# Gated decode attention with a GLU branch: where W_gate and W_up stand among the first loads

## The chip, the core and the metric

The kernel runs on one core of a Trainium2 chip. The metric is the device time of one execution in microseconds (us); lower is better. Three runs of the kernel before gave 1275.69, 1276.04 and 1276.13 us, a median of 1276.04 us.

## The reference

One token passes through two branches, and a scalar gate mixes them. All inputs are bfloat16.

```python
def _A_ref(x, k_cache, v_cache, wq, wo):      # x [1,1,448]; 16 query heads, 8 KV heads, Sk 65536, Dh 256
    q = (x @ wq).reshape(B, Sq, Hq, Dh).transpose(0, 2, 1, 3)
    ...                                       # each KV head serves 2 query heads
    scores = jnp.einsum("bhqd,bhkd->bhqk", q, k) * (Dh ** -0.5)
    p = _softmax(scores, axis=-1)
    o = jnp.einsum("bhqk,bhkd->bhqd", p, v)
    return o.transpose(0, 2, 1, 3).reshape(B, Sq, Hq * Dh) @ wo
def _B_ref(x, W_gate, W_up, W_down):          # W_gate, W_up [448,1792]; W_down [1792,448]
    gate = x @ W_gate; up = x @ W_up
    return (gate * (gate > 0) * up) @ W_down
g = _sigmoid((x * gate_w).sum(-1, keepdims=True))
return g * a + (1 - g) * b
```

The K and V caches hold 8 x 65536 x 256 values each, 537 MB together. Everything else is small beside them.

## The kernel before

**Tiles.** Each KV head h has four K tiles and four V tiles. A tile is 16384 rows of 256 values, laid out as 128 partitions by 32768 values, 8192 KB. In all there are 32 K tiles (k0 to k31, called n in the code) and 32 V tiles (v0 to v31).

**Three slots.** A tile fills one of three SBUF buffers, `ring[0]` to `ring[2]`. K tile n goes to slot 1 + n % 2. V tiles go to slot 0, apart from the last four. Slot 0 has other guests before v0 comes: the query weights (the load `wq`, in the two pieces L626 and L627), W_down behind them (`wd`, L675), and then, over the place of the query weights, W_gate and W_up (`gu`, two DMAs each, L640 and L642). A load into a slot waits for the last reader of what lay there (`free`): k2 waits for the scores of k0, k3 for those of k1, k4 for those of k2. The `gu` loads wait for the query projection `q`, which reads the query weights. v0 waits for the whole GLU branch, since `gu`'s data and its intermediate results lie in slot 0.

**One queue of loads.** All these loads are issued by SyncE (SP) in one fixed order. SP waits for the semaphores of one load, issues it, and goes on to the next; a load that waits holds up those behind it.

**Work on a tile.** For a K tile, VectorE transposes it in place in four steps (L529), TensorE multiplies each half with the query (`qk[n, 0]` and `qk[n, 1]`, L540), VectorE takes the maximum of the scores (L703), and ScalarE the exponential (L705). When the four K tiles of a head are done, the head's softmax factors follow (L715 to L760). For a V tile, ScalarE brings the tile's weights into place (`pc`, L591) and TensorE multiplies (`pv`, L584). The GLU branch runs once, after the scores of k2: the products with W_gate and W_up on TensorE (`f_gu`, L653), relu, product, transpose and cast on VectorE (L659, L660, L663, L664), and the product with W_down on TensorE (`f_dn`, L551 with `hT`, in the code `dn`).

**What sets the order.** A planner written by hand. The list `order` names the loads with an estimated duration each; their running sum gives each load a planned issue time `t` and a planned landing time `tL`. Each operation gets a key worked out from these times, and each engine's program is sorted by key. So the list sets the order on SP directly, and the order on the other engines by the keys. Dependencies become semaphore waits afterwards.

Of the kernel before, what the change touches and what calls it, by code (L numbers as in the profile page):

```python
# [27 lines left out]
class _Plan:  # L28
# [8 lines left out]
    def op(self, eng, key, fn, deps=(), tag=None):  # L37
        eng, cls = {"pv": ("pe", "pv"), "dx": ("dv", "dx"), "ap": ("ac", "ap")}.get(eng, (eng, eng))
        o = _Op(eng, key, fn, deps, tag=tag, cls=cls)
        self.ops.append(o)  # L40
        return o
# [219 lines left out]
def bass_gated_mix__gqa_block_cached__glu_gated_reglu__decode_kernel(  # L261
# [35 lines left out]
    with es:  # L297
# [73 lines left out]
        op, dma = pl.op, pl.dma  # L371
# [6 lines left out]


        TILE = 19.35  # L380
        order = [("k", 0, TILE), ("wq", 0, 8.7), ("k", 1, TILE), ("wd", 0, 3.8), ("k", 2, TILE), ("gu", 0, 7.7)]
        for n in range(3, NT):
            order.append(("k", n, TILE))
            if n >= NTH:
# [10 lines left out]
        t = 3.0  # L395
        tL, issue = {}, []
# [158 lines left out]
        def f_sel(e, win):  # L555
            for d_ in range(8):
                ins = e.matmul(AX_ps, win(d_), o_sb[:, d_ * 32:(d_ + 1) * 32],
                               start=False, stop=False, skip_group_check=True)
            return ins

        l_, qk, smax, aexp, pv, pc, last, first = {}, {}, {}, {}, {}, {}, {}, {}
# [8 lines left out]
        def zero_o(key, h):  # L570
            last["zo", h] = op("pv", key, lambda e: e.matmul(
                OP[:], identb[:, :], zer[:, 0:1].to_broadcast([128, 512]), start=True, stop=True, skip_group_check=True),
                [c_ze, g_idb, l_["hT"], last.get(("o1", h - 1))], tag="zo")

        def make_pv(n, lo, hi, sl, tv, dep):
            h, a = divmod(n, NTH)

            def f_pv(lo, hi):
                return lambda e: f_mm(e, lo, hi)

            def f_mm(e, lo, hi):
                for k in range(lo // 2, hi // 2):
                    g = k % 4
                    ins = e.matmul(OP[32 * g:32 * g + 4, :], pcur[a % 2][:, 4 * k:4 * k + 4],  # L584
                                   ring[sl][:, k * 512:(k + 1) * 512],
                                   start=False, stop=False, skip_group_check=True,
                                   tile_position=(0, 32 * g))
                return ins
            tp = max(tv, last["tev", h])
            if lo == 0:  # L590
                pc[n] = op("ap", max(tp - 5, last["tev", h] - 0.5), lambda e: e.copy(  # L591
                    pcur[a % 2][:].rearrange("p (k i) -> p k i", i=4),
                    ptp[:].rearrange("p (k i f) -> p k i f", i=4, f=4)[:, :, :, a]), last["ev", h] + [pv.get(n - 2)])
            if lo == 0 and a == 0:
                zero_o(last["tev", h] - 0.3, h)
            if n < NT - 1:
                pc[n].deps.append(dep)
            deps = ([dep] if n == NT - 1 else []) + [pc[n]] + ([last["zo", h]] if a == 0 and lo == 0 else [])
            if n >= NT - NTH and a == 1:
                for q_, (l2, h2) in enumerate(PIECES):  # L600
                    pv[n] = op("pv", tp + 0.1 * q_, f_pv(l2, h2), deps if q_ == 0 else [pc[n]], tag=("tail", 1, q_))
            else:
                tag = ("pv", a % 2, sl) if n < NT - NTH else ("tail", a % 2, 0 if n < NT - 1 else [q_[0] for q_ in PIECES].index(lo))
                pv[n] = op("pv", tp, f_pv(lo, hi), deps, tag=tag)
            if a == NTH - 1 and hi == U:
                tn = last["T", h + 1] + 18.5 if n < NT - 1 else tp + 1.2
                o1 = op("dx", tn, lambda e: e.tensor_scalar(o_sb[:], OP[:, 0:256], rcm[:, 0:1], None, ALU.mult),  # L607
                        [pv[n], last.get(("otr", h - 1)), last["rc", h]])
                last["ocp", h] = o1
                o1 = op("dx", tn + 0.05, lambda e: e.scalar_tensor_tensor(  # L610
                    o_sb[:], OP[:, 256:512], rcm[:, 1:2], o_sb[:], ALU.mult, ALU.add), [o1, last.get(("ec", h))])

                if h < H - 1:
                    o2 = op("pv", tn + 0.3, lambda e: f_sel(e, lambda d_: ecur[:, 7 - d_:135 - d_]),
                            [o1], tag="otr")
                else:
                    o2 = op("pv", tn + 0.5, lambda e: f_sel(e, lambda d_: esel[:, 120 - 16 * h - d_:248 - 16 * h - d_]),
                            [o1, g_es, l_["axz"]])
                if h < H - 1:
                    last["l5", h + 1].deps.append(o1)  # L620
                last["o1", h], last["otr", h] = o1, o2
                last["tn", h] = tn + 1

        for kind, i, t in sorted(issue, key=lambda q: q[0] != "wq"):
            if kind == "wq":
                l_["wq"] = dma("sp", t, "wq", lambda e: e.dma_start(wq3, A_wq[0:NR3, :].rearrange("(p k) n -> p (k n)", k=R3)))  # L626
                l_["wqh"] = dma("sp", t + 0.01, "wqh", lambda e: e.dma_start(wqh, A_wq[NR3:D, :].rearrange("r (t n) -> (r t) n", t=2)))  # L627
# [48 lines left out]
            elif kind == "k":  # L676
                n = i
                h, t_ = divmod(n, NTH)
# [29 lines left out]
                if t_ == NTH - 1:  # L708
# [18 lines left out]
                    for rd in range(2):  # L727
# [18 lines left out]
                        q = op("ac", tt + 1, f_ev, [p, pv.get((h - 1) * NTH - 1)])  # L746
# [18 lines left out]
                    for args in [p_ for p_ in pending if p_[0] // NTH == h]:  # L765
                        make_pv(*args)
                        pending.remove(args)
            elif kind in ("v", "vp"):
                if kind == "v":
                    n, lo, hi = i, 0, U  # L770
                    sl = slot["v", n]
                    dep = dma("sp", t, "r%d" % sl, lambda e, sl=sl, n=n: e.dma_start(ring[sl][:], v_src(n)), free(("v", n)))
                else:
                    n, (lo, hi) = NT - 1, PIECES[i]
                    sl = slot["vp", 0]
                    dep = dma("sp", t, ("wq", "wqh", "wd")[i], lambda e, sl=sl, n=n, lo=lo, hi=hi: e.dma_start(  # L776
                        ring[sl][:, lo * 256:hi * 256], v_src(n)[:, :, lo * 256:hi * 256]), free(("vp", 0)))
                args = (n, lo, hi, sl, tL[kind, i], dep)
                if ("tev", n // NTH) in last:
                    make_pv(*args)  # L780
                else:
                    pending.append(args)
            elif kind == "wo":
                lo, hi = WO[i]
                l_["wo", i] = dma("sp", t, "wo%d" % i, lambda e, lo=lo, hi=hi: e.dma_start(  # L785
                    wo_sb[:, lo:hi, :], A_wo.rearrange("(p s) n -> p s n", s=32)[:, lo:hi, :]), free(("wo", 0)))
# [89 lines left out]
```

## Time and profile before

| | |
|---|---|
| median of 3 runs | 1276.04 us (1275.69 to 1276.13) |
| span of the profiled execution | 1274.3 us |
| DMA: share of 16 engines' span, bytes, mean rate | 99.7%, 549.13 MB, 431 GB/s |
| VectorE (DVE) busy | 630.1 us (49%) |
| TensorE (PE) busy | 365.9 us (29%) |
| ScalarE (ACT) busy | 78.0 us (6%) |

The page gives the profiled execution's span and no other time of its own; the span is 1.7 us below the median of the three runs, and that difference lies around the span. Times within the profile are us from the start of the span. "DMA ring<-in_A_k_cache_dram" is the load of a K tile, "SPq" is SP's queue of DMA issues. The number that stands for a DMA "to landing" runs from the start of its issue until its semaphore shows that all of it has arrived. An entry in square brackets behind an instruction is the idle time of its engine before it, and what ended it.

### The profile page before, as it was taken

The numbers are of one execution on the slowest core, as the hardware profiler recorded it, in microseconds if no ns is written. First come the engines' busy times: TensorE is split into PE (matmuls) and PEld (weight loads), VectorE is DVE, ScalarE is ACT, GpSimd is POOL, SyncE is SP. The second block draws the span as 40 slices with busy tenths as digits, with TensorE's granted clock in tenths as the row PEclk, the third lists the DMA queues.
The fourth block names the chain that finished last, engine by engine and source line by source line (L and its number), as shares of the span: only waits on it lengthen the run. The fifth ranks groups of instructions, "written<-read, shape, count | busy, mean of one in ns | idle before, by whom it ended". The sixth has DMA issues, their size and how long they took to land.

```text
span 1274.3 us, 10240 instructions
## 1 busy us (share of the span) xinstructions
PE 365.9 (29%) x4497; PEld 151.4 (12%) x4505; DVE 630.1 (49%) x309; ACT 78.0 (6%) x163; POOL 4.6 (0%) x23
## 2 busy tenths in 40 slices
PE   0534321133320332312233222323302332112525
PEld 0101110011110111101111110111100111001201
DVE  4777655553455633557433565335654355553300
ACT  0001100010000100001000010000000010000100
POOL 1000000000000000000000000000000000000000
PEclk9766665666655666656666656666566666566667
DMA  9999999999999999999999999999999999999998
GB/s 411 430 436 432 426 430 434 432 443 432 430 432 432 434 442 430 430 434 430 438 438 430 430 434 430 440 438 428 430 434 430 444 434 428 430 436 430 442 421 369
DMA packets 11389, 549.13 MB, mean 431 GB/s; under 512 B 1267, under 2 KB 1654, under 8 KB 2294
## 3 DMA queue, kind: packets, MB, share of 16 engines
q1 hardware_dynamic: 11378, 549.03, 99.7%
q8 instruction: 4, 0.07, 0.0%
q14 instruction: 3, 0.02, 0.0%
q10 hardware_dynamic: 4, 0.00, 0.0%
HBM read 549.03 MB, written 0.00 MB: 431 GB/s over the span
## 4 chain that ended last, share of the span: by engine, by line
DMA 81%; PE 16%; DVE 2%; ACT 1%; issue 1%; SPq 0%; ACTq 0%
DMA ring<-in_A_v_cache_dram 74%; PE O L584 13%; DMA ring<-in_A_wo_dram 3%; DMA ring<-in_A_wq_dram 2%; DMA ring<-in_A_k_cache_dram 2%; DVE ring L529 1%; PE ST L540 1%; ACT pcur L591 1%; PE O L501 1%; PE A_ps L551 0%; SPq L785 0%; SPq L776 0%; PE O L653 0%; DVE ring L660 0%; PE A_ps L653 0%
## 5 line engine op out<-in xcount | busy, mean ns | idle before, releaser
L529 DVE STREAM_TRANSPOSE ring<-ring 128x4096 uint32<-128x4096 uint32 x128 | 557.6, 4413 | 196.9 <-DMA ring<-in_A_k_cache_dram 196.9
L584 PE MATMUL O<-ring,pcur 128*4 128x512 bf16 x2048 | 187.3, 545 | 790.4 <-ACT pcur L591 781.9
L703 DVE TENSOR_REDUCE nmb<-ST 128x1 f32<-128x512 f32 x32 | 22.1, 692 | 345.9 <-PE ST L540 345.9
L584 PEld LDWEIGHTS O<-ring,pcur 128*4 128x4 bf16 x2048 | 59.3, 111 | 914.8 <-ACT pcur L591 794.6
L540 PE MATMUL ST<-ring,xcur 128*16 128x512 bf16 x2048 | 136.7, 420 | 44.3 <-DVE ring L529 43.7
L540 PEld LDWEIGHTS ST<-ring,xcur 128*16 128x16 bf16 x2048 | 62.4, 92 | 112.1 <-DVE ring L529 48.6
L705 ACT ACTIVATE P_sb<-ST,nmb 128x512 bf16<-128x512 f32 x32 | 44.6, 1392 | 368.3 <-DVE nmb L703 368.3
L591 ACT COPY pcur<-ptp 128x256 bf16<-128x256 bf16 x32 | 13.2, 415 | 732.6 <-DMA ring<-in_A_v_cache_dram 732.6
L607 DVE TENSOR_SCALAR o_sb<-O,rcm 128x256 bf16<-128x256 f32 x8 | 3.8, 479 | 61.1 <-PE O L584 61.1
L730 DVE TENSOR_TENSOR P_sb<-P_sb,hs 128x1024 bf16<-128x1024 bf16 x16 | 18.9, 1222 | 8.1 <-ACT hs L724 8.1
L735 PE MATMUL PT<-identb,P_sb 128*128 128x128 bf16 x128 | 14.5, 282 | 17.6 <-DVE P_sb L730 17.3
L501 PE MATMUL O<-ring,P_sb 128*128 128x512 bf16 x28 | 8.5, 477 | 17.3 <-DMA ring<-in_A_wq_dram 17.3
L735 PEld LDWEIGHTS PT<-identb,P_sb 128*128 128x128 bf16 x128 | 10.7, 127 | 19.9 <-DVE P_sb L730 19.9
L744 ACT COPY ptp<-PT 128x256 bf16<-128x256 bf16 x32 | 10.3, 375 | 23.0 <-PE PT L735 23.0
L705 ACT ACTIVATION_READ_ACCUMULATOR P_sb<-ST,nmb 128x1 f32 x32 | 8.3, 258 | 0.0
L501 PEld LDWEIGHTS O<-ring,P_sb 128*128 128x128 bf16 x28 | 3.2, 117 | 22.2 <-issue 20.5
L551 PE MATMUL A_ps<-ring,attnA 128*1 128x224 bf16 x64 | 5.3, 322 | 1.1 <-DMA ring<-in_A_wo_dram 1.0
L719 PE MATMUL M_ps<-identf,hs 128*2 128x128 f32 x8 | 2.3, 283 | 10.0 <-DVE hs L717 10.0
L756 DVE RECIPROCAL rc<-M_ps 128x2 f32<-128x2 f32 x8 | 1.4, 171 | 7.5 <-PE M_ps L755 7.5
L755 PE MATMUL M_ps<-hs,ones_f 128*128 128x2 f32 x16 | 4.5, 352 | 0.0
L722 PE MATMUL M_ps<-mx,nselT 2*128 2x1 f32 x16 | 3.2, 268 | 3.0 <-DVE mx L721 3.0
L755 PEld LDWEIGHTS M_ps<-hs,ones_f 128*128 128x128 f32 x16 | 4.0, 311 | 0.0
(93 smaller groups left out, 68.6 us busy)
## 6 DMA issues: line engine op xcount, KB each, us to landing
ring<-in_A_v_cache_dram SPq DMA_DIRECT2D x1, 4096.0 KB, 22.1
ring<-in_A_wq_dram SPq DMA_DIRECT2D x1, 3072.0 KB, 28.9
ring<-in_A_v_cache_dram SPq DMA_DIRECT2D x1, 3072.0 KB, 28.8
ring<-in_B_W_down_dram SPq DMA_DIRECT2D x1, 1568.0 KB, 53.0
ring<-in_B_W_gate_dram SPq DMA_DIRECT2D x1, 1344.0 KB, 26.3
ring<-in_B_W_up_dram SPq DMA_DIRECT2D x1, 1344.0 KB, 29.2
ring<-in_A_wo_dram SPq DMA_DIRECT2D x1, 1232.0 KB, 33.0
ring<-in_A_v_cache_dram SPq DMA_DIRECT2D x1, 1024.0 KB, 30.7
```

What stands on the lines that cost most here:

```text
L501: ins = e.matmul(QN_ps, xw3[:, kt, 31 - m:159 - m], rhs, start=(kt == 0 and m == 0), stop=(kt == R3 and m == J // 4 - 1))
L529: return lambda e: e.transpose(v, v)
L540: ins = e.matmul(bank[32 * w:32 * w + 16, :], xcur[:, x0:x0 + 16], ktv[sl][:, u0:u0 + 16, c, :, r_], start=(b == 0 and c == 0 and r_ == 0) ...
L551: ins = e.matmul(A_ps[32 * g:32 * g + 1, 0:D2], lhsT, rhs[:, g * D2:(g + 1) * D2], start=start, stop=stop, skip_group_check=True, tile_pos ...
L584: ins = e.matmul(OP[32 * g:32 * g + 4, :], pcur[a % 2][:, 4 * k:4 * k + 4], ring[sl][:, k * 512:(k + 1) * 512], start=False, stop=False, s ...
L591: pc[n] = op("ap", max(tp - 5, last["tev", h] - 0.5), lambda e: e.copy(pcur[a % 2][:].rearrange("p (k i) -> p k i", i=4), ptp[:].rearrange ...
L703: smax[n] = op("dv", sx, lambda e, n=n, t_=t_: e.tensor_reduce(NM[:, t_:t_ + 1], ST[n % 2][:], AX.X, ALU.max, negate=True), [qk[n, 1], las ...
L705: aexp[n] = op("ac", sx + 1, lambda e, n=n, t_=t_: e.activation(P_sb[:, t_:2048:4], ST[n % 2][:], ACTF.Exp, bias=NM[:, t_:t_ + 1], scale=1 ...
L730: rsc = op("dv", tt, lambda e, pb=pb: e.tensor_tensor(pb, pb, X[:, 12:16].unsqueeze(1).to_broadcast([128, 256, 4]), ALU.mult), [h7, aexp[n]])
L735: ins = e.transpose(PT[rd][:, s * 128:(s + 1) * 128], P_sb[:, (rd * 8 + s) * 128:(rd * 8 + s + 1) * 128], identb[:, :])
L744: ins = e.copy(dst, src)
L755: l3 = mop("pe", T + 19, lambda e: e.matmul(LS_ps, ones_f[:, :], X[:, 6:8], start=True, stop=True), [l2, c_one], tag="l3")
```

## The change

W_gate and W_up are loaded ahead of the third K tile, k2; they came behind it. The list `order` says so. Two more lines keep the rest in place: the GLU operations are still created after k2's (so that they can refer to the scores of k2), and the first V tile's weight copy `pc[0]` gets a key that leaves it where it was on ScalarE.

```diff
-        order = [("k", 0, TILE), ("wq", 0, 8.7), ("k", 1, TILE), ("wd", 0, 3.8), ("k", 2, TILE), ("gu", 0, 7.7)]
+        order = [("k", 0, TILE), ("wq", 0, 8.7), ("k", 1, TILE), ("wd", 0, 3.8), ("gu", 0, 7.7), ("k", 2, TILE)]
...
-                pc[n] = op("ap", max(tp - 5, last["tev", h] - 0.5), lambda e: e.copy(
+                pc[n] = op("ap", max(tp - (5 if n else 1), last["tev", h] - 0.5), lambda e: e.copy(
...
-        for kind, i, t in sorted(issue, key=lambda q: q[0] != "wq"):
+        for kind, i, t in sorted(issue, key=lambda q: (q[0] != "wq", tL["k", 2] if q[0] == "gu" else q[2])):
```

On SP, the first loads of the program before stand as follows; k0 and the query weights are ahead of this piece, the first row is k1, and `s_pe` and `s_pv` are the semaphores of TensorE's score products and of its other products.

```order
L680 DMA ring<-in_A_k_cache_dram 128x32768
L675 DMA ring<-in_B_W_down_dram 128x6272
L680 DMA ring<-in_A_k_cache_dram 128x32768 [waits s_pe]
L640 DMA ring<-in_B_W_gate_dram 128x5376 [waits s_pv]
L642 DMA ring<-in_B_W_gate_dram 128x896
L640 DMA ring<-in_B_W_up_dram 128x5376
L642 DMA ring<-in_B_W_up_dram 128x896
L680 DMA ring<-in_A_k_cache_dram 128x32768 [waits s_pe] x2
L772 DMA ring<-in_A_v_cache_dram 128x1x32768 [waits s_pv]
```

The same piece of SP's program after the change:

```order
L680 DMA ring<-in_A_k_cache_dram 128x32768
L675 DMA ring<-in_B_W_down_dram 128x6272
L640 DMA ring<-in_B_W_gate_dram 128x5376 [waits s_pv]
L642 DMA ring<-in_B_W_gate_dram 128x896
L640 DMA ring<-in_B_W_up_dram 128x5376
L642 DMA ring<-in_B_W_up_dram 128x896
L680 DMA ring<-in_A_k_cache_dram 128x32768 [waits s_pe] x3
L772 DMA ring<-in_A_v_cache_dram 128x1x32768 [waits s_pv]
```

k2 has moved behind the four loads of W_gate and W_up; it is now the first of the three K tiles (k2, k3, k4) that stand in one row ahead of v0. Nothing else moves on SP.

On VectorE, the program from the maximum of k1's scores to the transposes of k3 is the same before and after the change (`d_r1` and `d_r2` are the landings in slots 1 and 2, `s_pv` at L659 the products with W_gate and W_up):

```order
L703 TENSOR_REDUCE nmb<-ST 128x1 [waits s_pe]
L529 STREAM_TRANSPOSE ring<-ring 128x4096 [waits d_r1]
L529 STREAM_TRANSPOSE ring<-ring 128x4096 [waits s_ac]
L529 STREAM_TRANSPOSE ring<-ring 128x4096 x2
L703 TENSOR_REDUCE nmb<-ST 128x1 [waits s_pe]
L659 TENSOR_SCALAR ring<-O 128x448 [waits s_pv]
L660 SCALAR_TENSOR_TENSOR ring<-ring,gb,A_ps 128x448 [waits s_dx]
L663 STREAM_TRANSPOSE ring<-ring 128x448 [waits s_dx]
L664 CAST hT<-ring 128x14 [waits s_dx]
L529 STREAM_TRANSPOSE ring<-ring 128x4096 [waits d_r2]
```

The first transposes are k2's, the last row is k3's first; the GLU steps stand between them, so they still run after the scores of k2, wherever their data has arrived by then. TensorE's and ScalarE's programs are also the same as before.

## The prediction

> **What bounds the kernel now.** I read the page first, for the share of each resource, and then SP's waits, the chain of waits, and the timelines of SP, DVE and PE over the first 160 us, where the change lies. From the page, the span, the DMA rate in 40 slices, and the queue that the loads use:
>
> ```profile
> span 1274.3 us, 10240 instructions
> GB/s 411 430 436 432 426 430 434 432 443 432 430 432 432 434 442 430 430 434 430 438 438 430 430 434 430 440 438 428 430 434 430 444 434 428 430 436 430 442 421 369
> q1 hardware_dynamic: 11378, 549.03, 99.7%
> ```
>
> The 16 DMA engines work for 99.7% of the span, and the rate is level from the second slice to the last but one. The kernel is a queue of loads that never runs dry. Its length is bytes by rate; other work counts only where it lets the queue run dry, and such a gap is then never made up, since no later stretch has spare rate. The change neither adds nor removes a byte. So there is one question: does the new order of issue open or close a gap?
>
> The table of windows gives the rate of the steady part (its last three columns are PE's granted clock, the DMA share and GB/s), and the chain of waits, below it, the pace of its tiles (start, duration):
>
> ```profile
> 141.10:1231.70 1090.60, 302.26 (x3915) 127.49 (x3922) 531.26 (x229) 66.76 (x140) 0.00 (x0) 0.62 1.00 434
> ```
>
> ```profile
> 141.18 0.43 ACT pcur L591
> ...
> 1224.80 0.42 ACT pcur L591
> ```
>
> The DMA share there is 1.00 and the rate 434 GB/s, so nothing can go faster there. Between v0's landing (the copy at 141.18) and v28's (1224.80) lie 28 pairs of a K and a V tile, so a pair takes 38.70 us and **one tile 19.35 us** of the queue.
>
> Next, SP's timeline: when each load is issued (start, duration of the issue).
>
> ```profile
> 0.72 0.42 SPq L680 DMA_DIRECT2D ring<-in_A_k_cache_dram  x1
> 2.71 0.53 SPq L675 DMA_DIRECT2D ring<-in_B_W_down_dram  x1
> 50.70 0.33 SPq L680 DMA_DIRECT2D ring<-in_A_k_cache_dram  x1
> 52.56 0.44 SPq L642 DMA_DIRECT2D ring<-in_B_W_up_dram  x1
> 73.23 0.33 SPq L680 DMA_DIRECT2D ring<-in_A_k_cache_dram  x1
> 96.48 0.33 SPq L680 DMA_DIRECT2D ring<-in_A_k_cache_dram  x1
> 104.18 0.64 SPq L772 DMA_DIRECT2D ring<-in_A_v_cache_dram  x1
> 123.51 0.34 SPq L680 DMA_DIRECT2D ring<-in_A_k_cache_dram  x1
> ```
>
> These are k0, W_down, k2, the last piece of W_up, k3, k4, v0 and k5. The DMA view, asked for the issue of one load at a time, gives the time from issue to landing; its rows for k0, W_down, the last piece of W_up, k2, k3 and k4 are:
>
> ```profile
> ring<-in_A_k_cache_dram SPq DMA_DIRECT2D x1, 22.1
> ring<-in_B_W_down_dram SPq DMA_DIRECT2D x1, 1568.0 KB, 53.0
> ring<-in_B_W_up_dram SPq DMA_DIRECT2D x1, 224.0 KB, 30.5
> ring<-in_A_k_cache_dram SPq DMA_DIRECT2D x1, 24.6
> ring<-in_A_k_cache_dram SPq DMA_DIRECT2D x1, 29.1
> ring<-in_A_k_cache_dram SPq DMA_DIRECT2D x1, 25.3
> ```
>
> Adding these to the issues: W_down lands at 55.7, k2 at 75.3, W_up at 83.1, k3 at 102.3 and k4 at 121.8. The steps after W_down are 19.6, 7.8, 19.2 and 19.5, each what its bytes need. So the queue is fed without a gap through this part, and the slack of a load is the time between its issue and the landing of the load ahead of it: k2 is issued 5.0 us before W_down lands, k3 9.9 us before W_up lands, and **k4 5.8 us before k3 lands** (102.3 less 96.48).
>
> What releases k4 is seen in the chain of waits (start, duration), and on DVE's timeline:
>
> ```profile
> 31.49 8.51 PE O L501 x28
> ...
> 50.70 24.64 DMA ring<-in_A_k_cache_dram
> 75.37 17.43 DVE ring L529 x4
> 92.85 3.59 PE ST L540 x30
> ...
> 101.00 0.18 DVE hT L664
> ...
> 104.18 36.90 DMA ring<-in_A_v_cache_dram
> ...
> 147.16 32.62 DMA ring<-in_A_v_cache_dram
> ```
>
> ```profile
> 96.49 0.69 DVE L703 TENSOR_REDUCE nmb<-ST 128x1 f32<-128x512 f32 x1 [3.70 <-PE ST L540]
> 102.40 17.42 DVE L529 STREAM_TRANSPOSE ring<-ring 128x4096 uint32<-128x4096 uint32 x4 [1.22 <-DMA ring<-in_A_k_cache_dram]
> 131.30 17.42 DVE L529 STREAM_TRANSPOSE ring<-ring 128x4096 uint32<-128x4096 uint32 x4
> ```
>
> k2 lands, four transposes take 17.4 us, the second half of its scores 3.6 us, and with that its slot is free and k4 is issued: 96.48 less 75.34, 21.1 us after the landing.
>
> **The change, part by part.**
>
> *W_gate and W_up go earlier.* They wait only for the query projection, whose 28 products end at 40.0 (31.49 and 8.51). Their four issues now run then, not from 51.08. SP has nothing to do until 50.70, so no other load is held up by that wait. k1 and W_down are in the queue until 55.7, so the four loads land behind them, at about 55.7 + 7.7 = 63.4. Nobody wants them then: the GLU products stand on PE behind k2's scores, as before. Gain: nothing, for nobody waited for them at 83.1 either; the products began as k2's scores ended.
>
> *k2 goes later.* It is still issued at 50.70, when k0's scores are done, but lies behind W_gate and W_up. It lands where W_up landed, at 83.1, which is **7.7 us later** (83.06 less 75.34; their 3136 KB at 434 GB/s would be 7.4).
>
> *k3 stays.* Its issue at 73.23 hangs on the scores of k1, which the change does not touch. It is now 9.8 us ahead of k2's landing, and lands at 102.3 as before, since the bytes ahead of it are the same.
>
> *k4 comes too late.* DVE is free for k2 at 83.1 (k1's scores, which need its transposes, were done when k3 was issued at 73.23), so the 21.1 us from landing to release are unchanged, and k4 is issued at 83.1 + 21.1 = **104.2**. The load before it, k3, has by then been complete since 102.3. Behind k4 on SP is v0, which waits for the GLU branch and can't fill the hole. The 5.8 us of slack have become a lack of 1.9 us, and the queue is empty.
>
> *What a load costs on an empty queue.* The lack is not all: a load that finds the queue empty first has to start, a cost that the queue hides elsewhere. The row nearest to it is k0's, the same transfer on an empty queue: 22.1 us from issue to landing, 2.75 more than its 19.35. The other bound is the smallest load in the trace, the output at the end of SP's timeline:
>
> ```profile
> 1273.11 0.32 SPq L798 DMA_DIRECT2D out_dram<-P_sb  x1
> ```
>
> From its issue to the end of the span are 1.2 us, a start and an arrival with nearly no data between. So k4 lands at 104.2 + 22.1 = 126.3, or at the earliest at 104.2 + 19.35 + 1.2 = 124.75, against 121.8 before: a loss of 4.5 us, or 3.0 at least. I take 4.5, because k0's row has the same shape and spreads over the same engines. At the program's start other things load too, which is why it may be a little high. More than 4.5 is open as well, since the 16 DMA engines do not finish k3 together. The DMA view of 98 to 106 us gives their rate in 40 steps of 0.2 us:
>
> ```profile
> GB/s 655 0 0 0 0 0 655 328 0 0 2622 983 655 0 0 0 0 0 655 328 0 0 1638 1638 983 0 0 0 0 0 655 328 0 0 1638 1638 655 328 0 0
> ```
>
> The packets come in clumps with a period of 2.4 us: a large one, and a small one some 1.4 us behind it. The engines of the large clump would wait 1.4 us longer than the last ones, on which the landings hang. If the late ones catch up by the end, up to 1.5 us more are lost; I allow that much above 4.5.
>
> The Trainium skill, in "DMA: Bandwidth & Descriptors", section "Anatomy of one DMA — SWDGE (gpsimd) path", puts the fixed part of a DMA at about 2.0 us, for another path of issue. With that figure the loss would be an estimated 1.9 + 2.0 = 3.9 us (the row of 7.7, the slack of 5.8), and the time 1279.9; the rows here bound that part by 1.2 and 2.75.
>
> *What follows is late but covered.* The GLU steps and W_down's product shift by 7.7, so v0 is issued at 111.9; k4 is in flight until 126.3, 14 us of cover. k3's transposes started at its landing, 102.40; now they start when DVE has done the GLU steps, 101.2 + 7.7 = 108.9, so k5's issue goes from 123.51 to 130.0; v0 is in flight until 126.3 + 19.35 = 145.7, so this is covered by 15 us. k4's transposes go from 131.30 to 137.8 and are over long before k5's data, at 165. From here each V load is issued with some 13 us of other loads ahead of it, as the steady part has it (v1's 32.62 us in the chain, less its own 19.35), so the shift dies out. No second gap opens.
>
> *Sum.* Against the profiled execution: 1274.3 + 4.5 = 1278.8 of span. The median lies 1.7 above the span, so 1276.0 + 4.5 = **1280.5 us**. About 0.2% (2.6 us) is what a measurement of this kernel can tell from no change; the loss lies above that at both bounds.
>
> **The rivals.**
>
> *A: no gap (not slower).* The slack of k4 is 5.8 us and the shift 7.7. If k2's way from landing to release were 1.9 us or more shorter, the issue would still come in time, and the time stay at 1276.0. For it: only 1.9 us decide, and PE's last 3.6 us need only be halved. Against: k3's way took 21.1 us too (102.40 to 123.51), and the larger part, DVE's transposes, keeps its time over the whole profile; the page's group has 4413 ns as the mean of 128, 17.65 us for four:
>
> ```profile
> L529 DVE STREAM_TRANSPOSE ring<-ring 128x4096 uint32<-128x4096 uint32 x128 | 557.6, 4413 | 196.9 <-DMA ring<-in_A_k_cache_dram 196.9
> ```
>
> Chance 0.09.
>
> *B: the whole shift comes through.* The chain of waits runs from k2 through the GLU branch to v0, and each piece of it is 7.7 us later; whoever takes the chain at its word adds 7.7: 1283.7. Against it: the chain's piece "DMA" for v0 is 36.90 us, of which 17.5 are waiting behind k4, and that is slack. It needs a second gap, as at v0 or k5, where I count 14 and 15 us of cover. Chance 0.06.
>
> *C: the early start pays.* Each of the four weight loads has a start like that of the output, 1.2 us; if these were exposed behind k2, and now hidden behind k1, four would be worth up to 4.8 us: 1271.2. Against it: W_up lands 7.7 us after k2 while the bytes need 7.4, so at most 0.3 us were exposed. Chance 0.05.
>
> The Trainium skill, in "DMA: Bandwidth & Descriptors", section "Rules for kernel authors", advises to issue a DMA early and to wait for it late, so that its setup is covered. By that rule the move would be for the better; what the rows above show is that these starts were covered already, behind k2.
>
> That the change does not do what it says is excluded by the order on SP.
>
> **How the numbers follow.** The forecast, one gap of 3.0 to 6.0 us ahead of k4, has a chance of 0.80, with 1280.5 as its time and 1279.0 to 1282.0 as its own range. The range given is widened below by 0.7 for a shorter way from landing to release and the spread of the runs, and above by 0.2 for the latter: 1278.3 to 1282.2. It leaves out A, B and C, 2 in 10 together. Faster: C, 0.05. Same: A and some small gap below 2.6 us, 0.09 + 0.03 = 0.12. Slower: the rest of the forecast and B, 0.77 + 0.06 = 0.83.
>
> **What would show it.** In the profile after: k2's landing (start of its transposes) at about 83.1; k3's issue still at 73.2; k4's issue at about 104.2; a hole of 3 to 5 us in the DMA windows between 100 and 108, which the trace of before doesn't have; v0's landing at 145 to 146 where it was 141.1; and from there every tile again at 19.35. If the hole is there and v0's landing is 4 to 5 us late, but the span is not, then the queue can make up time and my first step is wrong. If k4 is issued before 102, A holds. If v0's landing is 7 us late or later, look for the second gap, B.

## The result, and the profile after

The changed kernel takes 1281.34 us (median of 5 runs, 1281.18 to 1281.52) against 1275.92 (1275.69 to 1276.13) for the kernel before, run beside it: **5.4 us slower**, a ratio of 1.0042 with a 95% interval of 1.003 to 1.0055. The forecast was 1280.5, with 1278.3 to 1282.2 as its range.

The page of the kernel after, the same three rows as before the change:

```profile
span 1279.5 us, 10248 instructions
GB/s 410 439 430 365 425 428 434 449 426 428 426 451 432 426 428 443 440 426 428 428 451 430 426 428 445 438 426 428 430 449 430 426 428 445 438 426 428 430 435 365
q1 hardware_dynamic: 11378, 549.03, 99.3%
```

The same bytes, 5.2 us more of span. One slice of the 40 stands out: the fourth (96 to 128 us) has 365 GB/s where it had 432. The other differences between the two rows go up to 19 GB/s either way and cancel: the mean of the other 39 slices is 430.8 in both. So nearly all of the loss is in one place. The windows from 94 to 106 us, first of before, then of after (last three columns: PE's granted clock, DMA share, GB/s):

```profile
94.00:106.00 12.00, 7.51 (x85) 3.30 (x77) 6.71 (x6) 1.42 (x2) 0.00 (x0) 0.71 1.01 437
```

```profile
94.00:106.00 12.00, 6.94 (x76) 2.10 (x68) 6.75 (x3) 1.42 (x2) 0.00 (x0) 0.67 0.69 273
```

In these 12 us the queue moved at 273 GB/s instead of its usual 434; (434 - 273) / 434 of 12 us are 4.5 us of lost queue within this window.

SP's timeline of the kernel after, with the first of the four weight loads, k3, k4, v0 and k5, and DVE's timeline below it:

```profile
40.44 0.33 SPq L640 DMA_DIRECT2D ring<-in_B_W_gate_dram  x1
...
73.10 0.33 SPq L680 DMA_DIRECT2D ring<-in_A_k_cache_dram  x1
103.75 0.33 SPq L680 DMA_DIRECT2D ring<-in_A_k_cache_dram  x1
111.66 0.64 SPq L772 DMA_DIRECT2D ring<-in_A_v_cache_dram  x1
129.54 0.34 SPq L680 DMA_DIRECT2D ring<-in_A_k_cache_dram  x1
```

```profile
82.64 17.42 DVE L529 STREAM_TRANSPOSE ring<-ring 128x4096 uint32<-128x4096 uint32 x4 [8.84 <-DMA ring<-in_A_k_cache_dram]
103.75 0.69 DVE L703 TENSOR_REDUCE nmb<-ST 128x1 f32<-128x512 f32 x1 [3.70 <-PE ST L540]
...
108.57 17.41 DVE L529 STREAM_TRANSPOSE ring<-ring 128x4096 uint32<-128x4096 uint32 x4
```

The weights are issued 10.6 us earlier (40.44, before 51.08), and k2's transposes begin at 82.64 instead of 75.37, after 8.84 us in which DVE waited for k2. k3 is issued when it was, k4 7.3 us later, at 103.75. The DMA view gives 28.9 us from issue to landing for k3 and 21.9 for k4:

```profile
ring<-in_A_k_cache_dram SPq DMA_DIRECT2D x1, 28.9
...
ring<-in_A_k_cache_dram SPq DMA_DIRECT2D x1, 21.9
```

So k3 lands at 102.0, and k4's issue comes 1.75 us behind that. k4 lands at 125.65, 3.9 us later than before (121.8), although the kernel loses 5.4. Where the rest is shows in the DMA rate in steps of 0.25 us: first 92 to 102, then 104 to 114, both of the kernel after:

```profile
GB/s 0 524 1311 1311 262 0 262 0 0 524 0 786 2097 524 0 262 0 0 524 0 0 1311 1573 524 0 262 0 0 524 0 0 0 0 0 0 0 0 0 0 0
...
GB/s 0 0 1311 2097 524 262 0 0 0 0 0 0 0 0 262 1835 1573 524 0 0 0 0 0 0 786 2097 1049 262 0 0 0 0 0 0 1311 2097 786 0 0 0
```

Each clump is one packet on most of the 16 engines; up to the gap, the clumps follow each other every 2.4 us. The last large one lies at 97.4, the last small one behind it, of two engines, at 99.0. The next clump lies at 104.75, and now all 16 engines are in it. The one after it follows 3.0 us later, and from there it is 2.4 again. So the engines of the large clump lost 104.75 - 97.4 - 2.4 = 5.0 us, and 0.6 more for a slow first packet: 5.6. The late engines lost 104.75 - 99.0 - 2.4 + 0.6 = 3.95 us. A landing is the landing of the last engine, so k4's landing shows 3.9. Most engines lost 5.6: the 1.6 us by which they had been ahead of the last ones are gone too.

By v0 more of this can be read off a landing: ScalarE's copy for v0 starts at 146.16, where it was 141.18, 5.0 us later, and so it stays up to the last of these copies. The 1.1 us between k4's 3.9 and v0's 5.0 show in the DMA view of 124 to 134 us, again in steps of 0.25 us. One packet there belongs to another queue, q8:

```profile
GB/s 0 0 786 2097 1049 262 0 0 0 0 0 0 1311 2097 786 0 0 0 0 0 0 262 1835 1573 524 0 0 0 0 0 0 524 2163 1049 262 262 0 0 0 0
q8 instruction: 1, 0.02, 0.5%
```

The first three clumps are level, with all 16 engines within 1 us. In the clump at 132, with the q8 packet in it, are only 15 loads' packets; the sixteenth follows at 132.75 to 133, and behind each later clump one packet stays alone, about 1 us late, until v0 has landed. The kernel before has such a q8 packet at 131.6 too, but there the engine that falls back only joins the three that are behind anyway, and v0's landing does not move. So the head start of most engines was worth something: it hid this delay. The view does not name the engines; that the q8 packet held this one is read from the times, and no experiment tried it.

### The profile page after: what moved, and what is told of

It is laid out like the page before. It is cut to its first block, busy times and chain, and to the rows that moved or that the text cites. A ratio compares the mean times of both kernels' runs of the same rounds, so it can differ in the third digit from the quotient of the medians.

```text
span 1279.5 us, 10248 instructions
## 1 busy us (share of the span) xinstructions
PE 358.4 (28%) x4505; PEld 148.2 (12%) x4505; DVE 630.1 (49%) x309; ACT 77.9 (6%) x163; POOL 4.6 (0%) x23
## 4 chain that ended last, share of the span: by engine, by line
DMA 81%; PE 15%; DVE 2%; ACT 1%; issue 1%; SPq 0%; ACTq 0%
DMA ring<-in_A_v_cache_dram 74%; PE O L584 13%; DMA ring<-in_A_wo_dram 3%; DMA ring<-in_A_k_cache_dram 3%; DMA ring<-in_A_wq_dram 2%; DVE ring L529 1%; PE ST L540 1%; ACT pcur L591 1%; PE O L501 1%; PE A_ps L551 0%; SPq L776 0%; PE O L653 0%; SPq L785 0%; DVE ring L660 0%; PE A_ps L653 0%
## 5 line engine op out<-in xcount | busy, mean ns | idle before, releaser
L584 PE MATMUL O<-ring,pcur 128*4 128x512 bf16 x2048 | 178.4, 524 | 793.9 <-ACT pcur L591 785.8
L703 DVE TENSOR_REDUCE nmb<-ST 128x1 f32<-128x512 f32 x32 | 22.1, 692 | 336.5 <-PE ST L540 336.5
L571 PE MATMUL O<-zer,identb 128*128 128x512 bf16 x8 | 4.7, 587 | 0.0
L557 PE MATMUL A_ps<-o_sb,ecur 128*128 128x32 bf16 x64 | 3.2, 191 | 3.2 <-DVE o_sb L610 3.2
## 6 DMA issues: line engine op xcount, KB each, us to landing
ring<-in_A_wq_dram SPq DMA_DIRECT2D x1, 3072.0 KB, 28.9
```

The source lines that it names most:

```text
L571: last["zo", h] = op("pv", key, lambda e: e.matmul(OP[:], identb[:, :], zer[:, 0:1].to_broadcast([128, 512]), start=True, stop=True, skip_ ...
L703: smax[n] = op("dv", sx, lambda e, n=n, t_=t_: e.tensor_reduce(NM[:, t_:t_ + 1], ST[n % 2][:], AX.X, ALU.max, negate=True), [qk[n, 1], las ...
```

## The experiments

The theory: the whole loss is one gap in the queue of loads ahead of k4, since k4's issue hangs on k2's landing and comes too late. The rivals: the chain through the GLU branch to v0 carries the loss (B); or the new order of the loads costs as such. Each kernel was timed beside the kernel before (median 1275.89 and 1275.92 in the two sets).

**k4 late, loads in their old order.**

```diff
-                kd = dma("sp", t, ..., free(("k", n)))
+                kd = dma("sp", t, ..., free(("k", n)) + ([l_["dn"]] if n == 4 else []))
```

> The kernel before, all loads in their old order; only k4's issue also waits for the product with W_down (dn), which ends at 104.2 in the trace of before. So k4 is issued at 104.2 instead of 96.5, and k3's landing at 102.3 lies before it. Theory (one gap ahead of k4 is the whole loss): slower by 5 to 6 us, 1281 to 1282, as much as the change itself, with k2 still landing at 75.4. Rival (the new order of the loads costs, by late GLU steps or by small descriptors in another place): not slower, 1276.

Measured: 1280.47 us (1279.44 to 1282.29), ratio 1.0035 (1.0023 to 1.0047). The profiled execution took 1281.36. SP's timeline:

```profile
72.91 0.33 SPq L680 DMA_DIRECT2D ring<-in_A_k_cache_dram  x1
103.72 0.33 SPq L680 DMA_DIRECT2D ring<-in_A_k_cache_dram  x1
```

k4 is issued at 103.72, as in the changed kernel (103.75), and the time goes up by 4.6 us (5.5 in the profiled execution), with no load moved. The median is a little below the 1281 to 1282 expected, and the runs of this kernel scatter more than the others, over 2.9 us. So k4's lateness by itself makes a loss of about this size.

**GLU steps early.** In the changed kernel, the GLU branch is planned behind the scores of k1 instead of those of k2:

```diff
-                tg = max(tL["gu", 0] + 1, last["sx", 2] + 1)
-                last["free"] = tg + 0.6
+                tg = last["sx", 1] + 1
+                last["free"] = max(last["free"], tg)
...
-                km = [at(pv[NTH * (h - 1) + 2] if h else qk[2, 0]) for h in range(H)]
+                km = [at(pv[NTH * (h - 1) + 2] if h else l_["gu"]) for h in range(H)]
```

> The changed kernel, with the GLU steps (L653 to L664, and the product with W_down) moved ahead of k2's scores and transposes on TensorE and VectorE, so that they run at about 74 to 82, as soon as W_gate and W_up allow it. v0's issue still stands behind k4's on SP. Theory (gap ahead of k4): k4 is still issued at 103.7, when k2's scores are done; still slow, 1281 to 1281.5. Rival B (the chain through the GLU branch to v0 carries the loss): the chain is 7 us shorter, so the loss goes, 1276 to 1277.

Measured: 1281.60 us (1281.24 to 1281.96), ratio 1.0043 (1.0029 to 1.0057). Its chain of waits:

```profile
83.10 17.43 DVE ring L529 x4
100.53 0.04 issue
100.58 3.62 PE ST L540 x30
104.20 0.02 issue
104.22 0.33 SPq L680
104.54 0.04 issue
104.59 40.69 DMA ring<-in_A_v_cache_dram
```

The GLU branch has gone from the chain: v0 is issued 0.4 us behind k4, at 104.59 instead of 111.66. The time is that of the changed kernel to 0.3 us. Rival B falls: the path through the GLU steps carries none of the loss. What stays in the chain is k2, its transposes, its scores and k4's issue.

**Half the shift.** In the changed kernel, W_up goes behind k2 again:

```diff
-                    a1.append(dma("sp", t + 0.01 * i_, "r0", ...
+                    a1.append(dma("sp", (t, tL["gu", 0] + 0.02)[i_], "r0", ...
```

(and so for its second piece).

> The changed kernel with W_gate alone ahead of k2, W_up behind it again: half the shift. Theory: k2 lands 3.8 us later than before, at 79.1, k4 is issued at 100.2, about 2 us before k3's landing at 102.3. That is just enough or lacks a few tenths for the engines that finish k3 early: 1276.0 to 1276.8. Rival (the loss is in proportion to the shift, as when the chain carries it): half of 5.4, 1278.6.

Measured: 1277.58 us (1277.33 to 1277.99), ratio 1.0013 (1.0004 to 1.0022), a loss of 1.7 us. Neither expectation is right: less than half, but more than the theory had allowed. SP's timeline has k3 and k4:

```profile
73.17 0.33 SPq L680 DMA_DIRECT2D ring<-in_A_k_cache_dram  x1
100.11 0.33 SPq L680 DMA_DIRECT2D ring<-in_A_k_cache_dram  x1
```

k3 takes 29.0 us and lands at 102.2. k4 is issued 2.1 us *ahead* of that, and yet 1.7 us are lost. The window shows it too (94 to 106, as above):

```profile
94.00:106.00 12.00, 6.89 (x73) 2.56 (x75) 6.35 (x7) 1.41 (x2) 0.00 (x0) 0.69 0.89 360
```

360 GB/s instead of 434 are 2.0 us. k4's landing hardly shows it: 21.8 us behind its issue, k4 lands at 121.9, where it was 121.8. What went is again the head start of most engines: k4's first clump, at 101.0 to 101.75, has all 16 of them. An issue 2 us ahead of the landing of the load before it does not keep the queue full.

**W_down as a filler.** In the changed kernel, W_down's load goes between k3 and k4:

```diff
-                l_["wd"] = dma("sp", t, "wd", ...
+                l_["wd"] = dma("sp", tL["k", 2] + 0.02, "wd", ...
```

> The changed kernel with W_down's load moved from ahead of W_gate to between k3 and k4, where it needs no wait. Theory: its 3.8 us fill the hole; k2 lands at 79.3, k4 is issued at 100.4 and W_down lands at 102.3, so the slack is again about 2 us: 1276.0 to 1276.8, although W_gate and W_up stay ahead of k2. Rival (having W_gate and W_up ahead of k2 costs as such): 1281.3 as the changed kernel, or 1281 plus what the product with W_down waits.

Measured: 1277.67 us (1277.19 to 1277.93), ratio 1.0013 (1.0004 to 1.0022), 1.8 us lost. k4 is issued at 100.01, and W_down lands at 73.28 + 28.7 = 101.98; the lead is 2.0 us, the loss that of the kernel before this one. W_gate and W_up still stand ahead of k2, so their place as such accounts for at most this 1.8 of the 5.4 us. The theory's price for a short lead was too low a second time, and the next three kernels measure it.

**Three leads.** The kernel before, with k4's issue held by an operation that ends earlier or later: the cast `hT`, the relu, or the first transpose of k3 (for the last, k4's key on SP is also put off, behind that transpose; k4 still stands ahead of v0).

```diff
-                kd = dma("sp", t, ..., free(("k", n)))
+                kd = dma("sp", t, ..., free(("k", n)) + ([l_["hT"]] if n == 4 else []))
```

> The kernel before; only k4's issue also waits for the cast hT (L664), which ends at 101.2 in the trace of before: 1.1 us ahead of k3's landing at 102.3. Theory now (a gap, and a start that needs about 3.7 us of lead, as the issues at 103.7, 100.1 and 100.0 with losses of 5.4, 1.7 and 1.8 give it): loss 3.7 - 1.1 = 2.6 us, 1278.5. Rival (what counts is whether the issue comes ahead of the landing, with a start of 1 to 2 us): loss 0.1 to 0.9, 1276.0 to 1276.8.

> The kernel before; only k4's issue also waits for the relu (L659), which ends at 99.3 in the trace of before, 3.0 us ahead of k3's landing. Theory (3.7 us of lead needed): loss 0.7 us, 1276.6. Rival (an issue ahead of the landing costs nothing beyond its start of 1 to 2 us): no loss, 1275.9.

> The kernel before; only k4's issue also waits for the first transpose of k3, which ends at 106.8 in the trace of before, 4.5 us after k3's landing. Theory (loss = 3.7 us less the lead, and no cover used up behind it): 3.7 + 4.5 = 8.2 us, 1284.1. Rival (the queue makes up part of a longer gap later, or a fixed cost of any gap of about 5.4 us): 1281 to 1282.

Measured: 1278.10 us (1277.37 to 1278.73), 1277.27 us (1275.86 to 1278.08) and 1284.06 us (1283.91 to 1284.93); ratios 1.0017 (1.0008 to 1.0026), 1.0010 (1.0001 to 1.0019) and 1.0064 (1.0050 to 1.0077). SP's timeline has k4's issue at 100.14, 98.47 and 107.16:

```profile
100.14 0.33 SPq L680 DMA_DIRECT2D ring<-in_A_k_cache_dram  x1
```

```profile
98.47 0.33 SPq L680 DMA_DIRECT2D ring<-in_A_k_cache_dram  x1
```

```profile
107.16 0.33 SPq L680 DMA_DIRECT2D ring<-in_A_k_cache_dram  x1
```

With the lead taken from each kernel's own profile (landing of the load ahead, less k4's issue), all kernels of this study but the last one below stand in one table:

| kernel | k4 issued | load ahead landed | lead, us | median loss, us | 3.7 - lead |
|---|---|---|---|---|---|
| before | 96.48 | 102.3 | 5.85 | 0 | 0 |
| k4 waits for relu | 98.47 | 102.1 | 3.6 | 1.35 | 0.1 |
| W_gate only | 100.11 | 102.2 | 2.1 | 1.7 | 1.6 |
| k4 waits for hT | 100.14 | 102.2 | 2.0 | 2.2 | 1.7 |
| W_down behind k3 | 100.01 | 102.0 | 2.0 | 1.8 | 1.7 |
| after | 103.75 | 102.0 | -1.75 | 5.4 | 5.45 |
| k4 waits for dn | 103.72 | 102.0 | -1.7 | 4.6 | 5.4 |
| GLU steps early | 104.22 | 102.4 | -1.8 | 5.7 | 5.5 |
| k4 waits for k3's transpose | 107.16 | 102.6 | -4.6 | 8.1 | 8.3 |

The 3.7 was taken from three of these kernels (after, W_gate only, W_down behind k3), which therefore fit it; the others test it. From a lead of 2 us down to a lack of 4.6, each us of lead that goes costs about 1 us, whatever took it away, and nothing of a long gap is made up later. The kernel with k4 behind dn lies 0.8 us off, within its scatter. The one with hT had 2.0 us of lead instead of the 1.1 planned, and so lost 2.2 us instead of the 2.6 expected.

The kernel that waits for the relu misses the line: it should lose 0.1 us (0.7 was expected) and loses 1.35, with single runs from 1275.86 to 1278.08. Its window from 94 to 106:

```profile
94.00:106.00 12.00, 5.32 (x81) 2.44 (x73) 7.04 (x6) 1.41 (x2) 0.00 (x0) 0.91 1.04 431
```

The engines did not stand still: their share is 1.04, where it was 1.01 before the change, but with it they moved only 431 GB/s instead of 437. The same bytes took 4% more of the engines' time, 0.5 us of these 12. So the gap is closed at this lead, and some slow packets remain; ScalarE's copy for v0 starts 0.85 us late. The end of the line is not sharp, and the lead that is enough lies between 3.6 and 5.85 us.

**Using the early weights.** In the changed kernel with the GLU steps early, v0's issue also goes ahead of k4's, since slot 0 is free by 80:

```diff
-                    dep = dma("sp", t, ...
+                    dep = dma("sp", t if n else tL["k", 3] - 0.01, ...
```

> The changed kernel with the GLU steps ahead of k2's scores and transposes, and v0's issue moved ahead of k4's: v0 can be issued at about 82, when the product with W_down is done, 20 us ahead of k3's landing. Theory: no gap ahead of v0, and k4, issued at 103.7, has v0's 19 us as cover: the whole loss goes, 1275.9 (1275.3 to 1276.5); the queue was full before, so there is little to win beyond. Rival (W_gate and W_up ahead of k2 cost as such): 1281.

Measured: 1275.84 us (1275.76 to 1276.04), ratio 1.0000 (0.9991 to 1.0009). SP's timeline and the window from 94 to 106:

```profile
80.21 0.64 SPq L772 DMA_DIRECT2D ring<-in_A_v_cache_dram  x1
103.88 22.05 SPq L680 DMA_DIRECT2D ring<-in_A_k_cache_dram  x2
```

```profile
94.00:106.00 12.00, 4.76 (x44) 1.11 (x36) 8.30 (x4) 1.39 (x2) 0.00 (x0) 0.58 1.01 437
```

k4 is issued as late as in the changed kernel, but v0 is in the queue behind k3, 22 us ahead of k3's landing (102.1), and the rate is 437 GB/s as before the change. W_gate and W_up are where the change put them, and the loss is zero. So their place costs nothing as such. It is no faster than the kernel before either: the queue was full there, and a better cover has nothing to win.

## Why the prediction was right, point by point

*A full queue decides, and a gap is not made up.* Shown: the losses grow with the lack up to 8.1 us, and the rate behind the gap is what it was.

*The weights gain nothing by going earlier.* Shown by the last kernel: even with their early use, 1275.84.

*k2 7.7 us late, k4 issued at 104.2.* 7.3 us (82.64 less 75.37) and 103.75. The 21.1 us from landing to release stayed 21.1 (82.64 to 103.75). The lack was 1.75 us, forecast 1.9.

*The cost of an empty queue.* This term was mis-sized. I priced it by landings: 4.5 us, with k0's 22.1 us. By landings it came to 3.9, with 21.9 us for k4 and its issue 0.45 us earlier than forecast. But the loss is 5.4, since the landing follows the last engines: most engines had finished k3 about 1.6 us ahead of these, and lost this head start too, which one engine's delay of 1.1 us by v0 then made visible. The prediction had this effect only as 1.5 us of allowance above its value; it belonged into the value, and without the allowance the measured time would lie outside the range. The two errors, 0.6 us too much by landings and the head start left out, partly cancelled, which is luck. Its evidence, the clumps, was already in the trace of before. With the large clump as the measure, the sum is the 1.75 us of lack and 3.8 for the restart: 2.2 from the end of that clump's last packet (97.4 + 2.4 = 99.8) to the landing at 102.0, 1.0 from k4's issue at 103.75 to its first clump at 104.75, and 0.6 for the slow first packet.

The Trainium skill's fixed part of about 2.0 us for a DMA ("DMA: Bandwidth & Descriptors", section "Anatomy of one DMA — SWDGE (gpsimd) path") would have given an estimated 3.9 us. The measured 5.4 decide: a fixed part by itself does not hold the uneven end of the engines.

*What follows is covered.* Shown: v0 was issued at 111.66 (forecast 111.9) and k5 at 129.54 (130.0), and neither opened a gap.

*Rivals.* A (no gap) fell with k4's issue at 103.75. B fell with the GLU steps moved early, with no effect on the time. C (an early start pays) fell with the last kernel. The rule of the Trainium skill to issue a DMA early ("DMA: Bandwidth & Descriptors", section "Rules for kernel authors") did not help here: in one queue in order, a load that nobody waits for pushed back a load on which the next issue depended, and that cost 5.4 us.

*Left open.* That the packet of q8 made the 1.1 us between k4's and v0's landing was read from one trace and not tried. Why the first packets behind an empty queue are slower is not known, nor where the last 0.4 us between v0's 5.0 and the kernel's 5.4 went, nor why the kernel that waits for the relu scatters by 2.2 us.

## What to carry to other kernels

In a kernel bound by one queue of loads, read for each load the lead: the landing of the load ahead of it less its own issue. Before moving a load, follow the tile that it pushes back to the issue that this tile's slot releases, and ask for nearly 6 us of lead there, not for zero: here 5.85 us lost nothing, and 3.6 us still lost 1.35. Here the early load cost nothing once its early use freed a slot and the load for that slot was issued early too, to cover the gap; it won nothing either, for the queue had been full before.

## What the runs showed of the hardware

The 16 engines do not finish a tile together: in this trace, most were some 1.6 us ahead of the last ones, whose arrival the semaphore shows. After an empty queue, the second packets came 3.0 us behind the first instead of 2.4. Behind one packet of queue q8 (0.02 MB), one engine was about 1 us late, and stayed so up to v0's landing. Together, a load of 8 MB had to be issued more than 3.6 us before the landing of its predecessor to cost nothing; with a lead of 2.0 us the kernels lost 1.7 to 2.2.
